# A linear-attention kernel with a sine-gated feed-forward: alpha's load on another queue, w_in in other pieces, the opening's copies and batch 1's steps dealt out anew

## The chip, the cores and the metric

The kernel runs on one core of a Trainium2 chip. A core has five engines that run side by side, each through its own list of instructions in order: TensorE (PE in the profile; PEld is its loading of weights), VectorE (DVE), ScalarE (ACT), GpSimd (POOL) and SyncE (SP). They wait for each other through semaphores. SP, ACT and POOL can also issue DMA transfers, which 16 DMA engines carry out. The metric is the device time of one execution in microseconds (us). Times inside the execution are counted from the start of the profiled span.

## The reference

```python
def _attn_ref(q, k, v):                       # batch 8, heads 8, sequence 576, head_dim 64
    q_s = softmax of q over head_dim          # exp, then divided by the sum over the last axis
    k_s = softmax of k over the sequence
    kv = np.einsum('bhsd,bhse->bhde', k_s, v)
    return np.einsum('bhsd,bhde->bhse', q_s, kv)

def _moe_ref(x, w_in, w_out, alpha):          # 4608 tokens, d_model 512, d_ff 2048
    h = x @ w_in
    s = np.sin(alpha * h)
    g = h + s * s / (alpha + 1e-09)
    return g @ w_out
```

The first function's result, its heads side by side, gives the 4608 x 512 tokens x of the second. All inputs and the output are float32; the matmuls run in bfloat16.

## The kernel before, in words

A batch's 576 tokens lie on 64 partitions with 9 tokens (j) each; two heads share the 128 partitions, so q, k and v of a batch are tiles of 128 x 4 x 9 x 64. They are loaded and worked on in two halves of the heads (ii = 0, 1).

For each batch ACT takes the exponentials of q and k (`exp_half`, `exp_q`, `exp_k`, L119), one engine casts v to bfloat16 beside a column of ones (`cast_v0`, `cast_v1`, `cast_v`), and q is normalized by sums (tensor_reduce, reciprocal) and a product (`norm_q0`, `norm_q`). TensorE multiplies k and v (`kv_mm`, L174, 36 small matmuls for a half), DVE divides by the column that the ones gave (`kv_norm`, L184 and L185: kvr, kbd), TensorE turns q over (`q_transpose_ii`, L201: tp) and multiplies it with kv (`attn_x`, L218). The result is copied to xT, tokens along the free axis.

The feed-forward runs over 9 tiles of 512 tokens. For each of 16 blocks of 128 hidden columns, `mm_h` (L263) adds four matmuls, over four blocks of 128 rows of w_in in the order KO = 0, 2, 1, 3. `sine` (L269) makes sin(alpha h) on ACT; the square is taken by ACT (A, L271), POOL (P, L273) or DVE (D, L275), and `combine` (L279) on DVE adds it to h and writes g. Then `mm_o` (L283) multiplies g and w_out, 64 matmuls a tile, and `evac_o` (L295, L298) copies the sums and stores them.

The order on each engine is the order of the lines, written by hand (`manual_schedule`). PSUM banks come from pools named by letters: a, b and l of two banks each, and k of one double one. A bank is written anew when its last reader is done.

In the opening SP issues q, k, q, v, k of batch 0 (L308, halves), ACT alpha (L313). POOL waits for k's first half (the copy `held`, L340), issues v's second half in two pieces (5 and 4 of the 9 tokens), w_in in six ranges of columns, each by two DMAs of 64 partitions (`load_win`, L109), and the first half of w_out (L112); these DMAs cast float32 to bfloat16. TensorE runs warm-up matmuls until there is work. Then comes tile 0, which needs batch 0 alone. Within its 16 blocks, SP and POOL issue the later loads (`late`, L455): after block 6 q's first half of batch 1, after 8 and 10 w_out's blocks 8 to 12 and 12 to 14, after 13 q's second half and k and v of batch 1. A one-column copy on DVE (L443) to the tile that q's load overwrites keeps that load from starting sooner.

The 64 output matmuls of tile 0 (`o_quad`) are an iterator; `take(os, n)` lets the next n run. Batch 1's attention steps stand between them: `norm_q` (first product on POOL, L153, second on DVE), `held` and w_out's blocks 14 to 16 behind it (L469, L470), the casts of v (first half on ACT, second on DVE, L474), two `transpose_q1` (L482), two `kv_mm` with `kv_norm`, two `x_half` (L491). DMAs of each batch's ninth token of q (q8, L497) and of batch 2 follow. From tile 1 on the order is the same before and after the change.

Of the kernel before, what the change touches and what calls it, by code (L numbers as in the profile page):

```python
# [15 lines left out]
F32 = mybir.dt.float32  # L16
# [7 lines left out]
def kernel(  # L24
# [14 lines left out]
    nc = tc.nc  # L39
# [41 lines left out]
    win_v = moe_w_in.rearrange("(c x d) n -> x d c n", x=2, c=4)  # L81
# [24 lines left out]
    def load_win(c0, c1, k0=0, k1=4):  # L106
        n, kk = slice(c0, c1), slice(k0, k1)
        for x in range(2):
            nc.gpsimd.dma_start(out=win[64 * x:64 * x + 64, kk, n], in_=win_v[x][:, kk, n])  # L109
# [88 lines left out]
    def q_transpose_ii(b, ii, j0, j1, tp):  # L198

        for j in range(j0, j1):  # L200
            nc.tensor.transpose(tp[:, j - j0], A["qn", b][:, ii, j], identb)  # L201
# [111 lines left out]
    nc.scalar.dma_start(out=alpha_rows, in_=moe_alpha.rearrange("(no ni) -> no ni", ni=128))  # L313
# [14 lines left out]
    tpa = warm[:, 0, 0:nN]  # L328
    nc.tensor.transpose(tpa, alpha_rows, ident[0:nN, 0:nN])
    DVE_CP(alpha_sb, tpa)  # L330
    nc.vector.reciprocal(inva_sb, alpha_sb)
# [3 lines left out]
    def cast_v0(ii, j0, j1, eng):  # L335
        vv = vb[0].rearrange("p j (i c) -> p i j c", i=4)
        eng(vv[:, 2 * ii:2 * ii + 2, j0:j1, 0:D], staged["v", 0][:, ii::2, j0:j1])
# [5 lines left out]
    for c0, c1 in ((0, 256), (256, 512), (512, 768), (768, 1024), (1024, 1536), (1536, 2048)):  # L343
        load_win(c0, c1)
# [3 lines left out]
    def warm_up(n):  # L348

        for _ in range(n):  # L350
            nc.tensor.matmul(warm, identb, A["qe", 0][:, 0:4, 0:128], start=True, stop=True)
# [32 lines left out]
    warm_up(1)  # L384
    kv_norm(0, 0, 1)
    tp1 = ps_l.tile([128, 8, 128], BF16, name="tp", tag="l")
    q_transpose_ii(0, 1, 0, 8, tp1)
    cast_v0(1, 0, 5, DVE_CP)
    cast_v0(1, 5, 9, ACT_CP)
# [3 lines left out]
    DVE_CP(xT[:, 0, 0:MF], xp[0])  # L393
    ACT_CP(xT[:, 2, 0:MF], xp[1])
    ACT_CP(A["qT", 0][:, 1, 0:8], tp1)
    nc.scalar.activation(zero, zero, AX.Sin)
    kv_mm(0, 1, ps_k, split=True)
    kv_norm(0, 1, 2)
    for ki in range(2):
        for ni in range(2):  # L400
            mm_h(0, ni, ki, ki + 1)
    xp = [bank("l") for _ in range(2)]
    attn_x(0, 1, 0, 8, xp)
    for x in range(2):
        DVE_CP(xT[:, 2 * x + 1, 0:MF], xp[x])
    for ki in range(2):
        for ni in range(2, 4):
            mm_h(0, ni, ki, ki + 1)
# [29 lines left out]
    with ES:  # L438
# [16 lines left out]
        late = {6: lambda: load_q1(0), 8: lambda: load_wout(8, 12), 10: lambda: load_wout(12, 14), 13: lambda: (load_q1(1), load_kv1())}  # L455
# [9 lines left out]
        take(os, 46)  # L465
        for ii in range(2):
            exp_half("q", 1, ii, 8)
        norm_q(1, [GP, V], 8)
        GP_CP(held, staged["k", 1][:, 0, 0, 0:1])  # L469
        load_wout(14, 16)  # L470

        def cast_v1(ii, eng):
            vv = vb[1].rearrange("p j (i c) -> p i j c", i=4)
            eng(vv[:, 2 * ii:2 * ii + 2, :, 0:D], staged["v", 1][:, ii::2])  # L474

        exp_half("k", 1, 0)
        cast_v1(0, ACT_CP)
        exp_half("k", 1, 1)
        def transpose_q1(ii):
            tp = ps_h[0].tile([128, 8, 128], BF16, name="tp", tag="a")  # L480
            q_transpose_ii(1, ii, 0, 8, tp)
            DVE_CP(q_tile(1)[:, ii, 0:8], tp)  # L482

        transpose_q1(0)
        take(os, 4)
# [6 lines left out]

        kv_mm(1, 0, ps_k, split=True)
        kv_norm(1, 0, 1)
        for b in range(2):
            DVE_CP(q8[:, 0, b, 0:1], zero)
            nc.sync.dma_start(out=q8[:, :, b], in_=src_view(q, b)[:, :, 8 * D:J * D])  # L497
        load_batch(2)
        cast_v1(1, DVE_CP)
        take(os, 4)  # L500
        x_half(0)
        take(os, 2)
        transpose_q1(1)
        kv_mm(1, 1, ps_k, split=True)
        kv_norm(1, 1, 2)
        take(os, 5)
# [186 lines left out]
```

## Time and profile before

| what | us |
|---|---|
| median of 3 runs (lowest, highest) | 283.63 (282.67, 283.71) |
| the profiled execution, its own time | 283.53 |
| its span, first to last instruction | 281.7 |
| TensorE busy | 268.6 |
| ACT, DVE, POOL busy | 224.1, 185.4, 83.5 |
| TensorE busy in 0 to 14 us | 8.08 |
| in 14 to 20 us | 5.71 |
| in 35 to 40 us | 4.35 |
| in 40 to 45 us | 4.39 |
| in 45 to 50 us | 5.00 |

```profile
PE   2999989999999999999999999999999999999994
DMA  7999989996699129811991199125011111111143
```

These two lines cut the span into 40 slices of 7.04 us. A digit is the busy share of a slice in tenths, 9 for 90% or more: for TensorE above, for the mean of the 16 DMA engines below. The granted clock of TensorE was 1.00 throughout. DMA lines in this document give the time from a DMA's issue to its landing; "KB" of a casting load counts the bfloat16 that it writes, half of what it reads.

### The profile page before, as it was taken

Reading aid. Unit: us, or ns where it says so; the run is one execution under the profiler, and the core shown is the slowest. Engines: PE = TensorE matmul, PEld = TensorE weight load, DVE = VectorE, ACT = ScalarE, POOL = GpSimd, SP = SyncE. Lnnn points to the kernel's source line nnn. Section 1 sums busy time; section 2 is a strip of 40 time slices with the busy share of each in tenths; the row PEclk is TensorE's granted clock in tenths of the full one; section 3 lists DMA queues with packets and bytes.
Section 4 is the critical chain, followed back from the end, with each engine's and each line's share of the span. In section 5 each row is a group of like instructions: output and inputs, shape, how many; then the busy total and the mean of one; then the engine's idle time right before and its main releaser. Section 6 shows DMA issues by size and latency. Waiting matters only on the chain.

```text
span 281.7 us, 4930 instructions
## 1 busy us (share of the span) xinstructions
PE 268.6 (95%) x1890; PEld 124.2 (44%) x1919; DVE 185.4 (66%) x280; ACT 224.1 (80%) x320; POOL 83.5 (30%) x80
## 2 busy tenths in 40 slices
PE   2999989999999999999999999999999999999994
PEld 1444444444444444444544444444444444444443
DVE  3868658799868767766866677567675555555412
ACT  4989466999588999899989998999877777777400
POOL 1989410777666550115003500341000000000000
PEclk9999999999999999999999999999999999999999
DMA  7999989996699129811991199125011111111143
GB/s 260 308 187 230 296 288 310 360 329 252 142 171 396 62 61 326 316 37 40 277 381 43 37 249 403 32 57 123 1 36 40 37 37 37 40 38 42 41 106 74
DMA packets 39128, 45.82 MB, mean 163 GB/s; under 512 B 17072, under 2 KB 22464, under 8 KB 39104
## 3 DMA queue, kind: packets, MB, share of 16 engines
q1 hardware_dynamic: 33360, 40.57, 46.6%
q0 software_dynamic: 5552, 4.79, 10.2%
q8 instruction: 15, 0.25, 0.3%
q10 hardware_dynamic: 192, 0.14, 0.2%
q14 instruction: 9, 0.07, 0.1%
HBM read 36.71 MB, written 9.44 MB: 164 GB/s over the span
## 4 chain that ended last, share of the span: by engine, by line
PE 85%; DMA 5%; DVE 4%; ACT 2%; issue 2%; POOL 1%; SPq 0%; ACTq 0%
PE op L283 38%; PE hp L263 37%; DMA st_v<-in_v_dram 3%; PE kvp L174 2%; PE lp L263 2%; DMA st_q<-in_q_dram 1%; POOL s L273 1%; PE op L263 1%; PE op L663 1%; ACT s L269 1%; PE hp L218 1%; PE kvp L263 1%; DVE qs L364 1%; DVE qn L366 1%; PE xp L218 1%
## 5 line engine op out<-in xcount | busy, mean ns | idle before, releaser
L279 DVE SCALAR_TENSOR_TENSOR g<-s,inva_sb,hp 128x512 bf16<-128x512 f32 x128 | 94.5, 745 | 58.8 <-ACT s L271 53.3
L263 PE MATMUL hp<-xT,win 128*128 128x512 bf16 x505 | 127.4, 379 | 0.7 <-DVE kvr L184 0.3
L283 PE MATMUL op<-wout,g 128*128 128x512 bf16 x478 | 121.0, 379 | 1.6 <-issue 1.1
L269 ACT ACTIVATE s<-hp,alpha_sb 128x512 f32<-128x512 f32 x128 | 86.2, 682 | 23.3 <-PE hp L263 21.9
L263 PEld LDWEIGHTS <-win 128*128 128x128 bf16 x576 | 55.9, 98 | 68.0 <-issue 1.7
L283 PEld LDWEIGHTS <-g 128*128 128x128 bf16 x560 | 53.2, 98 | 64.7 <-issue 2.3
L271 ACT ACTIVATE s<-s 128x512 f32<-128x512 f32 x112 | 70.5, 630 | 3.6
L273 POOL TENSOR_TENSOR s<-s 128x512 f32<-128x512 f32 x29 | 30.1, 1056 | 21.8 <-ACT s L269 21.8
L153 POOL TENSOR_TENSOR qn<-qe,qs 128x1152 bf16<-128x1152 bf16 (+1 forms) x12 | 25.1, 2111 | 34.0 <-DVE qs L147 25.3
L295 DVE COPY o<-op 128x512 f32<-128x512 f32 (+2 forms) x33 | 21.8, 660 | 10.2 <-PE op L283 7.9
L138 POOL CAST vb<-st_v 128x1152 bf16<-128x1152 f32 x12 | 14.7, 1259 | 44.7 <-DMA st_v<-in_v_dram 44.7
L119 ACT ACTIVATE qe<-st_q 128x1152 bf16<-128x1152 f32 (+2 forms) x18 | 17.7, 1024 | 6.2 <-DMA st_q<-in_q_dram 6.0
L119 ACT ACTIVATE ke<-st_k 128x1152 bf16<-128x1152 f32 x16 | 17.9, 1151 | 0.9 <-DMA st_k<-in_k_dram 0.9
L146 DVE TENSOR_REDUCE qs<-qe 128x36 f32<-128x2304 bf16 x5 | 12.8, 2551 | 8.3 <-ACT qe L119 8.3
L119 ACT ACT_TABLE_LOAD x7 | 9.0, 1283 | 1.3 <-PEq L677 1.2
L283 PE MATMUL hp<-wout,g 128*128 128x512 bf16 x31 | 8.8, 379 | 0.1
L283 PE MATMUL lp<-wout,g 128*128 128x512 bf16 x30 | 8.6, 380 | 0.2 <-issue 0.2
L174 PEld LDWEIGHTS <-ke 64*64 64x64 bf16 x576 | 5.8, 106 | 5.3 <-issue 2.1
L174 PE MATMUL kvp<-vb,ke 64*64 64x65 bf16 x576 | 6.9, 194 | 1.1 <-ACT vb L474 0.8
L263 PE MATMUL lp<-xT,win 128*128 128x512 bf16 x31 | 7.5, 379 | 0.1
L109 POOL DMA_DIRECT2D win<-in_moe_w_in_dram x12 | 7.4, 701 | 0.0
L231 DVE CAST xT<-xp 128x1024 bf16<-128x1024 f32 (+1 forms) x7 | 7.4, 1065 | 0.0
(86 smaller groups left out, 133.5 us busy)
## 6 DMA issues: line engine op xcount, KB each, us to landing
out_dram<-o SPq DMA_DIRECT2D x70, 128.0 KB, 2.4
st_q<-in_q_dram SPq DMA_DIRECT2D x6, 1152.0 KB, 6.2
st_k<-in_k_dram SPq DMA_DIRECT2D x6, 1152.0 KB, 8.6
st_v<-in_v_dram SPq DMA_DIRECT2D x6, 1152.0 KB, 11.1
st_k<-in_k_dram SPq DMA_DIRECT2D x4, 576.0 KB, 7.3
st_q<-in_q_dram SPq DMA_DIRECT2D x4, 512.0 KB, 5.9
st_v<-in_v_dram SPq DMA_DIRECT2D x3, 576.0 KB, 8.7
wout<-in_moe_w_out_dram POOLq DMA_DIRECT2D x3, 512.0 KB, 10.4
```

Of the source, the lines that this page charges most:

```text
L119: nc.scalar.activation(dst[:, :, ii * 128:(ii + 1) * 128].rearrange("p j (x d) -> p x j d", x=2), src[:, ii::2], AX.Exp)
L138: engs[ii](vv[:, 2 * ii:2 * ii + 2, :, 0:D], staged["v", b][:, ii::2])
L146: nc.vector.tensor_reduce(qs, A["qe", b].rearrange("p j (i d) -> p j i d", i=4), axis=AXL.X, op=ALU.add)
L153: engs[ii % len(engs)].tensor_tensor(qn[:, ii, 0:j1].rearrange("p j (x d) -> p j x d", x=2), qe[:, ii], part.unsqueeze(3).to_broadcast([12 ...
L174: nc.tensor.matmul(kvp[64 * x:64 * x + 64, e, ii * 65:(ii + 1) * 65], ke[r, j, h * 64:(h + 1) * 64], vt[r, j, h * 65:(h + 1) * 65], start= ...
L263: nc.tensor.matmul(hp, win[:, KO[k], ni * 128:(ni + 1) * 128], xT[:, KO[k], t * MF % NX:t * MF % NX + MF], start=(k == 0), stop=(k == 3))
L269: nc.scalar.activation(s, hp, AX.Sin, scale=alpha_sb[:, ni:ni + 1])
L271: nc.scalar.activation(s, s, AX.Square)
L273: nc.gpsimd.tensor_tensor(s, s, s, op=ALU.mult)
L279: nc.vector.scalar_tensor_tensor(G[t][:, ni], in0=s, scalar=inva_sb[:, ni:ni + 1], in1=hp, op0=ALU.mult, op1=ALU.add)
L283: nc.tensor.matmul(acc, G[t][:, ni, j * 128:(j + 1) * 128], wout[:, ni, :], start=(ni == 0), stop=(ni == nN - 1))
L295: eng(o[:, cols], acc)
```

## The change

Four things are changed.

- Alpha's load is issued by SP after the five loads of batch 0, where ACT issued it first. Its transpose on TensorE moves from the start to behind the third group of warm-up matmuls, its copy from DVE to ACT, and the reciprocal (inva_sb) to behind `kv_norm` of the second half.
- w_in comes by 128 partitions in 8 DMAs: rows' blocks 0 and 2 of columns 0 to 256 and 256 to 512, then blocks 1 and 3 of columns 0 to 512, then all rows of four ranges of 256 columns and of the last 512. The first matmuls of tile 0 follow that: block of columns 0 and 1 with row block 0, block 0 with row block 2, and behind `attn_x` of the second half the five others of blocks 0 to 3.
- In the opening both pieces of v's second half are cast by DVE, and DVE also copies q's second transposes; ACT copies both x of the first half and one of the second, and loads the sine's table after that.
- For batch 1, each half of v is cast by ACT (5 tokens) and POOL (4). q is normalized on DVE alone, its transposes come after 42 output matmuls (46 before) and ahead of the second half of v, and all steps are placed anew between the output matmuls. q's second half, k and v are loaded after block 12 of tile 0 (13 before).

```diff
@@ -78,7 +78,7 @@
     def src_view(t, b):
         return t[b].rearrange("(i e) (p j) d -> (e p) i (j d)", e=2, j=J)
 
-    win_v = moe_w_in.rearrange("(c x d) n -> x d c n", x=2, c=4)
+    win_v = moe_w_in.rearrange("(c p) n -> p c n", c=4)
     wout_v = moe_w_out.rearrange("(no ni) d -> ni no d", ni=128)
     out_v = out.rearrange("(b p j) d -> b j p d", b=B, j=J)
 
@@ -103,10 +103,8 @@
         load("k", k, b)
         load("v", v, b)
 
-    def load_win(c0, c1, k0=0, k1=4):
-        n, kk = slice(c0, c1), slice(k0, k1)
-        for x in range(2):
-            nc.gpsimd.dma_start(out=win[64 * x:64 * x + 64, kk, n], in_=win_v[x][:, kk, n])
+    def load_win(c0, c1, cc=slice(0, 4)):
+        nc.gpsimd.dma_start(out=win[:, cc, c0:c1], in_=win_v[:, cc, c0:c1])
 
     def load_wout(n0, n1):
         nc.gpsimd.dma_start(out=wout[:, n0:n1, :], in_=wout_v[:, n0:n1, :])
@@ -310,7 +308,7 @@
 
     for n, t, ii in (("q", q, 0), ("k", k, 0), ("q", q, 1), ("v", v, 0), ("k", k, 1)):
         load0(nc.sync, n, t, ii, 0, 8 if n == "q" else J)
-    nc.scalar.dma_start(out=alpha_rows, in_=moe_alpha.rearrange("(no ni) -> no ni", ni=128))
+    nc.sync.dma_start(out=alpha_rows, in_=moe_alpha.rearrange("(no ni) -> no ni", ni=128))
     make_identity(nc, ident)
     DVE_CP(identb, ident)
     zero = singles.tile([128, 1], F32, name="zero")
@@ -325,10 +323,6 @@
 
     tp0 = ps_h[0].tile([128, 8, 128], BF16, name="tp", tag="a")
     warm = ps_h[0].tile([128, 4, 128], F32, name="warm", tag="a")
-    tpa = warm[:, 0, 0:nN]
-    nc.tensor.transpose(tpa, alpha_rows, ident[0:nN, 0:nN])
-    DVE_CP(alpha_sb, tpa)
-    nc.vector.reciprocal(inva_sb, alpha_sb)
 
 
 
@@ -340,8 +334,12 @@
     GP_CP(held, staged["k", 0][:, 0, 0, 0:1])
     load0(GP, "v", v, 1, 0, 5)
     load0(GP, "v", v, 1, 5, 9)
-    for c0, c1 in ((0, 256), (256, 512), (512, 768), (768, 1024), (1024, 1536), (1536, 2048)):
-        load_win(c0, c1)
+    for c in range(2):
+        load_win(256 * c, 256 * c + 256, slice(0, 4, 2))
+    load_win(0, 512, slice(1, 4, 2))
+    for c in range(2, 6):
+        load_win(256 * c, 256 * c + 256)
+    load_win(1536, 2048)
     for c in range(2):
         load_wout(4 * c, 4 * c + 4)
 
@@ -382,30 +380,32 @@
     warm_up(2)
     kv_mm(0, 0, ps_k, split=True)
     warm_up(1)
+    tpa = warm[:, 0, 0:nN]
+    nc.tensor.transpose(tpa, alpha_rows, ident[0:nN, 0:nN])
     kv_norm(0, 0, 1)
     tp1 = ps_l.tile([128, 8, 128], BF16, name="tp", tag="l")
     q_transpose_ii(0, 1, 0, 8, tp1)
+    ACT_CP(alpha_sb, tpa)
     cast_v0(1, 0, 5, DVE_CP)
-    cast_v0(1, 5, 9, ACT_CP)
+    cast_v0(1, 5, 9, DVE_CP)
+    DVE_CP(A["qT", 0][:, 1, 0:8], tp1)
 
     xp = [bank("b") for _ in range(2)]
     attn_x(0, 0, 0, 8, xp)
-    DVE_CP(xT[:, 0, 0:MF], xp[0])
-    ACT_CP(xT[:, 2, 0:MF], xp[1])
-    ACT_CP(A["qT", 0][:, 1, 0:8], tp1)
-    nc.scalar.activation(zero, zero, AX.Sin)
+    for x in range(2):
+        ACT_CP(xT[:, 2 * x, 0:MF], xp[x])
     kv_mm(0, 1, ps_k, split=True)
     kv_norm(0, 1, 2)
-    for ki in range(2):
-        for ni in range(2):
-            mm_h(0, ni, ki, ki + 1)
+    nc.vector.reciprocal(inva_sb, alpha_sb)
+    for ni, ki in ((0, 0), (1, 0), (0, 1)):
+        mm_h(0, ni, ki, ki + 1)
     xp = [bank("l") for _ in range(2)]
     attn_x(0, 1, 0, 8, xp)
     for x in range(2):
-        DVE_CP(xT[:, 2 * x + 1, 0:MF], xp[x])
-    for ki in range(2):
-        for ni in range(2, 4):
-            mm_h(0, ni, ki, ki + 1)
+        (ACT_CP, DVE_CP)[x](xT[:, 2 * x + 1, 0:MF], xp[x])
+    nc.scalar.activation(zero, zero, AX.Sin)
+    for ni, ki in ((1, 1), (2, 0), (2, 1), (3, 0), (3, 1)):
+        mm_h(0, ni, ki, ki + 1)
 
     def h_slot(t, ni, sq, lag):
         hp = mm_h(t, ni, 2 if ni < (4, 1, 0)[min(t, 2)] else 0)
@@ -452,7 +452,8 @@
                     nc.sync.dma_start(out=staged[n, 1][:, ii::2].rearrange("p i j d -> p i (j d)"),
                                       in_=src_view(t, 1)[:, ii::2])
 
-        late = {6: lambda: load_q1(0), 8: lambda: load_wout(8, 12), 10: lambda: load_wout(12, 14), 13: lambda: (load_q1(1), load_kv1())}
+        late = {6: lambda: load_q1(0), 8: lambda: load_wout(8, 12), 10: lambda: load_wout(12, 14),
+                12: lambda: (load_q1(1), load_kv1())}
         for ni in range(nN):
             h_slot(0, ni, "DPPAPPAPPAAPPAPD"[ni], lag)
             flush(lag, 1)
@@ -462,27 +463,16 @@
 
         accs = [bank(kind) for kind in "bbll"]
         os = o_quad(0, accs, [DVE_CP, ACT_CP, DVE_CP, DVE_CP])
-        take(os, 46)
-        for ii in range(2):
-            exp_half("q", 1, ii, 8)
-        norm_q(1, [GP, V], 8)
-        GP_CP(held, staged["k", 1][:, 0, 0, 0:1])
-        load_wout(14, 16)
-
-        def cast_v1(ii, eng):
+
+        def cast_v1(ii):
             vv = vb[1].rearrange("p j (i c) -> p i j c", i=4)
-            eng(vv[:, 2 * ii:2 * ii + 2, :, 0:D], staged["v", 1][:, ii::2])
-
-        exp_half("k", 1, 0)
-        cast_v1(0, ACT_CP)
-        exp_half("k", 1, 1)
-        def transpose_q1(ii):
+            for j0, j1, eng in ((0, 5, ACT_CP), (5, 9, GP_CP)):
+                eng(vv[:, 2 * ii:2 * ii + 2, j0:j1, 0:D], staged["v", 1][:, ii::2, j0:j1])
+
+        def transpose_q1(ii, eng):
             tp = ps_h[0].tile([128, 8, 128], BF16, name="tp", tag="a")
             q_transpose_ii(1, ii, 0, 8, tp)
-            DVE_CP(q_tile(1)[:, ii, 0:8], tp)
-
-        transpose_q1(0)
-        take(os, 4)
+            eng(q_tile(1)[:, ii, 0:8], tp)
 
         def x_half(ii):
             xp = [bank("a") for _ in range(2)]
@@ -490,20 +480,46 @@
             for x in range(2):
                 (ACT_CP, DVE_CP)[x](xT[:, 2 * x + ii, MF:2 * MF], xp[x])
 
+        def q1_sums(ii):
+            part, src = qs1[:, :, 2 * ii:2 * ii + 2], qe1[:, ii]
+            nc.vector.tensor_reduce(part, src, axis=AXL.X, op=ALU.add)
+            nc.vector.reciprocal(part, part)
+
+        def q1_norm(ii):
+            part = qs1[:, :, 2 * ii:2 * ii + 2]
+            nc.vector.tensor_tensor(A["qn", 1][:, ii, 0:8].rearrange("p j (x d) -> p j x d", x=2), qe1[:, ii],
+                                    part.unsqueeze(3).to_broadcast([128, 8, 2, D]), op=ALU.mult)
+
+        take(os, 42)
+        for ii in range(2):
+            exp_half("q", 1, ii, 8)
+        qe1 = A["qe", 1][:, 0:8].rearrange("p j (ii x d) -> p ii j x d", ii=2, x=2)
+        A["qn", 1] = att1.tile([128, 2, J, 2 * D], BF16, name="qn")
+        qs1 = small.tile([128, 8, 4], F32, name="qs1")
+        GP_CP(held, staged["k", 1][:, 0, 0, 0:1])
+        load_wout(14, 16)
+        q1_sums(0)
+        q1_norm(0)
+        q1_sums(1)
+        exp_half("k", 1, 0)
+        cast_v1(0)
+        transpose_q1(0, DVE_CP)
+        exp_half("k", 1, 1)
+        q1_norm(1)
+        take(os, 10)
         kv_mm(1, 0, ps_k, split=True)
         kv_norm(1, 0, 1)
+        transpose_q1(1, DVE_CP)
         for b in range(2):
             DVE_CP(q8[:, 0, b, 0:1], zero)
             nc.sync.dma_start(out=q8[:, :, b], in_=src_view(q, b)[:, :, 8 * D:J * D])
         load_batch(2)
-        cast_v1(1, DVE_CP)
+        cast_v1(1)
         take(os, 4)
         x_half(0)
-        take(os, 2)
-        transpose_q1(1)
         kv_mm(1, 1, ps_k, split=True)
         kv_norm(1, 1, 2)
-        take(os, 5)
+        take(os, 4)
         x_half(1)
         exp_to(A["qe", 1][:, J - 2:J], q8)
         nc.scalar.activation(zero, zero, AX.Sin)
```

## The prediction

> **What bounds the kernel now.** I read the busy times first, then the chain in order of time, then the timeline of TensorE where it has holes, and last the DMA shares of those stretches.
>
> ```profile
> PE 268.6 (95%) x1890; PEld 124.2 (44%) x1919; DVE 185.4 (66%) x280; ACT 224.1 (80%) x320; POOL 83.5 (30%) x80
> 30.30 8.71 DMA st_v<-in_v_dram
> 39.03 1.18 ACT vb L474
> 38.81 0.59 PE L283 MATMUL hp<-wout,g 128*128 128x512 bf16 x2
> 40.25 0.48 PE L174 MATMUL kvp<-vb,ke 64*64 64x65 bf16 x36 [0.85 <-ACT vb L474]
> 42.02 0.77 DVE L474 CAST vb<-st_v 128x1152 bf16<-128x1152 f32 x1 [0.62 <-DMA st_v<-in_v_dram]
> 43.26 0.48 PE L174 MATMUL kvp<-vb,ke 64*64 64x65 bf16 x36
> 45.85 0.38 PE L263 MATMUL kvp<-xT,win 128*128 128x512 bf16 x1
> ```
>
> TensorE is busy 95% of the span. Matmuls of 512 columns start 0.216 us apart when nothing waits (16 from 28.00 to 31.45), and from 45.85 on they do so almost without a break; the end (266 to 281.7) is one accumulation and a store. So the change can win only before 45.85: in the opening, and in batch 1's part (37 to 46 us), where TensorE runs dry from 39.24 (38.81 plus two starts) to 40.25 and loses about 0.8 us more up to 45.85. The chain blames v of batch 1: first half landed at 39.01, second at 42.00.
>
> ```profile
> core 0: us, PE busy (x) PEld busy (x) DVE busy (x) ACT busy (x) POOL busy (x), PEclk, DMA share, GB/s
> 11.00:17.00 6.00, 5.15 (x66) 2.38 (x67) 3.67 (x9) 5.07 (x8) 5.93 (x10) 1.00 1.37 178
> 18.00:26.00 8.00, 7.95 (x38) 3.62 (x37) 6.95 (x11) 7.85 (x14) 7.16 (x8) 1.00 1.24 205
> 29.00:32.00 3.00, 3.00 (x16) 1.36 (x14) 3.00 (x7) 2.69 (x3) 0.89 (x1) 1.00 1.24 209
> 33.00:39.00 6.00, 5.95 (x34) 2.94 (x34) 2.85 (x5) 2.22 (x2) 2.86 (x3) 1.00 1.05 406
> ```
>
> The last two columns are the point. The DMA engines' share is over 1 from 3 us to 41 us: first q, k, v of batch 0, then w_in, w_out 0 to 8, w_out 8 to 14 with batch 1's loads behind them. (GB/s counts bytes written, so a casting load of 205 reads 410.) The issue time in the chain, 30.30, is then not the cause; the bytes ahead are.
>
> **The opening.** Alpha's load leaves ACT (issue 0.46 us at 0.74) for the sixth place on SyncE. ACT gains nothing: its first exponential waits for q, landed 4.91. Alpha (8 KB) now lands behind the second k half (10.50), by my estimate at 10.6; its transpose stands after the last warm-up matmul (10.81, 0.39 long), so the wait is nothing and the price is one 0.25 us matmul ahead of q's second transposes, 0.1 us net since those waited for DVE until 11.20. At worst it lands with the second v piece (11.95): 0.75.
>
> ```profile
> 13.10 1.02 ACT L395 COPY qT<-tp 128x1024 bf16<-128x1024 bf16 x1
> 14.34 0.41 PE L218 MATMUL lp<-qT,kbd 64*64 64x512 bf16 x4
> 14.79 1.29 DVE L405 CAST xT<-lp 128x512 bf16<-128x512 f32 x2 [1.14 <-PE lp L218]
> 17.64 1.03 PE L263 MATMUL kvp<-xT,win 128*128 128x512 bf16 x4
> ```
>
> DVE: the 640-wide v cast ends at 12.26 as before; the 512-wide one (its 640 took 0.74, so 0.6) to 12.85; qT copy 0.69 (row L482, same shape) to 13.54; kvr and kbd 0.45 to 14.0. ACT: k until 12.22, alpha 0.2, two xT copies of 0.58 to 13.6. Then x of the second half starts at 14.2 instead of 14.34, its two copies run side by side (ACT to 15.2, DVE to 15.35) instead of 1.29 on DVE, and the five matmuls in between end at 15.7. The next eight need the w_in piece of rows 1 and 3, fourth in POOL's queue: by the landings of before (12.57, 13.25, then 1.29 for 512-wide columns) about 14.6. So column block 4 starts at 15.7 + 8 x 0.216 = 17.4, 0.2 earlier than 17.64. ACT's table load moves from 14.15 to 15.2 and ends, with the dummy sine, at 16.7; the first sine at 16.55 becomes 16.7. Cover: the combine of block 12 ends at 29.28 and TensorE wants its bank at 29.73, 0.45 ahead; 0.2 + 0.15 fit. Bounds: -0.45 to +0.75, most likely -0.2.
>
> w_in: 12 issues (0.69 us each) become 8 of 0.66 to 0.8 (w_out's, with as many rows, take 0.81), so POOL is through a us sooner, and waits for ACT's sines at 17.90 anyway. Of its bytes 0.26 MB (512 rows x 256 columns x 2) go from the rate of 512-wide columns (205) to that of 256-wide (178): 0.2 us more of a full DMA.
>
> **Batch 1, the loads.** q's second half, k and v are issued after block 12 instead of 13: their gate (L443, 29.20) now follows block 11's combine (ends 28.28), so about 28.5, with ACT's shift: 0.8 earlier, five DMAs on SyncE, nothing else queued there. Their price lies between -0.8 (they land earlier by all of it) and +0.2 (a full DMA serves the same bytes, w_in costing 0.2 more). By the share of 1.24 in 29 to 32 us I take +0.2: second v half 42.2, first 39.2.
>
> **Batch 1, the work.** q's first product moves from POOL (1.91 us) to DVE (1.22), between the sums: ready at 34.6, transposed after 42 matmuls of the output instead of 46 (36.9 instead of 37.9); no wait. The second product starts when the copy of the first transposes is done, 38.6 to 39.8. v's halves are split, ACT 640 wide (between 0.61 for 512 and 1.17 for 1152: 0.72), POOL 512 wide (1.17 for 1152 undisturbed, so 0.55). Here DVE and POOL meet:
>
> ```profile
> 67.89 1.97 DVE L153 TENSOR_TENSOR qn<-qe,qs 128x1152 bf16<-128x1152 bf16 x1
> 68.59 3.40 POOL L138 CAST vb<-st_v 128x1152 bf16<-128x1152 f32 x2
> ```
>
> This product takes 1.38 alone (1.22 x 9/8) and here waited for POOL's until 68.6; POOL's first cast took 2.29 instead of 1.17, from 68.59 to 70.88, one us beyond DVE's end. So POOL's first piece waits for DVE until 39.8 and ends at 40.4, against ACT's 39.9: 0.5 us on the first kv product, which ends at 40.7.
>
> The Trainium skill has this as a rule against the change ("SBUF — State Buffer", section "SBUF: two separate sides"): a DVE instruction with two SBUF inputs and a GpSimd one hold a shared port pair exclusively, and the loser fully blocks. The rows above agree. By the rule both halves could lose; but beside the second v half DVE has only copies out of PSUM, so the sum would stay at the 0.5 already in it.
>
> Then q's second transposes 0.45 (41.2), their copy on DVE to 42.1, four matmuls to 42.05, x 0.35: TensorE is ready for the second kv product at 42.5. It needs v: 42.2 + 0.04 + 0.72 = 42.96. From there kv 0.41, four matmuls 0.86, x 0.35, four 0.86: 2.48, and block 0 of the next tile starts at 45.45 instead of 45.85. All that was in between 42 and 45.85 (two matmuls, second transposes, a wait of 0.14 for the xT copy) is done before v. The last w_out piece (issued at 36.93 behind `held`, 6.1 us to landing, 43.07) gets no earlier in a full DMA, 43.3, and is wanted at 43.37: it covers, barely, and caps any further gain.
>
> **The sum.** 0.40 us won at 45.85. The opening's 0.2 is lost in the wait for v, as would be a loss there up to 0.46. Downstream: q8's loads are issued 0.5 later (behind the qT copy on DVE), land near 45.3, and ACT reads them at 45.5 (45.79 before); batch 2's loads follow 0.5 later and are used from 61 us on. Nothing else moves. The profiled execution took 283.53 (span 281.7 and 1.8 around it); its median of runs is 283.63. 283.53 - 0.40 = 283.1.
>
> **The rivals.**
> - Issue bound. If v lands 0.8 earlier with its issue, as the chain has it, the second kv product starts when TensorE is ready, 42.5, or 42.1 if POOL is not blocked: 282.7 to 282.3. For it: SyncE's loads had 395 of 401 GB/s at 33 us, so they may push w_out 12 to 14 (wanted at 38.6, landed 34.45) behind them. Against it: the share over 1 throughout.
> - The last w_out piece ahead of v (slower). Its issue hangs on k's first half; if that comes earlier by passing w_out, 0.5 MB of reads enters POOL's queue while v's second half is under way, and costs at most 1.28 us at 410 GB/s, of which some 0.4 is paid now. Second v half 42.9, next tile 46.2: 283.9. It decides from a landing of 42.6 on.
> - No effect: v's cast and the opening save what the extra w_in time and POOL's block cost, 283.5.
> - The opening breaks: alpha or the ACT shift cost more than the 0.66 that is covered in all; 0.75 and a stalled bank would give 284 to 285.
>
> The Trainium skill speaks for the second ("DMA: Bandwidth & Descriptors", section "Queues, rings and completion order"): an engine goes round robin over the queues that have work. By it the sum would be near 283.9. No window here isolates that order.
>
> **How the numbers follow.** Forecast (282.8 to 283.5, with no effect in it) 0.55; issue bound 0.20; w_out ahead of v 0.17; opening 0.08. The range takes in 282.3 below and 283.9 above, and the 0.1 to 0.4 by which single runs of before differ (282.67 to 283.71): 282.2 to 284.3. A measurement tells 0.5% (1.4 us) from no change; the whole hole is about that, so faster by more 0.08 (from the first rival, with luck in the runs), slower by more 0.11 (the last and the worst of the second), within 0.81.
>
> **What would show it.** Right: kv of batch 1 waits for ACT's cast of v near 43.0 and block 0 of tile 1 starts near 45.4; v's second half lands at 42.0 to 42.4; POOL's first cast takes over 0.9. Wrong: v lands near 41.2, or after 42.6; TensorE waits for alpha; a stall for banks at 20 to 30 us.

## The result, and the profile after

The changed kernel takes 282.62 us (median of 22 runs, 282.06 to 283.69) where the kernel before took 283.56 on the same chip (22 runs): a ratio of 0.9963, interval 0.9949 to 0.9977. On another chip the pair gave 282.66 (12 runs) and 282.82 (35), ratio 0.9989 (0.9971 to 1.0007), which takes in no change. So it is faster by 0.4% on the first chip, and by a tenth of a per cent that the noise covers on the other; both are within the half per cent that the prediction called no change. What differs between the chips is the kernel before: 283.56 on the first, 282.82 to 282.86 on three others. The profiled execution of the changed kernel took 282.79 us, 0.74 less than that of before; its span is 280.98 (281.73 before). That execution of before (283.53), from which the prediction starts too, lies at the first chip's median and 0.7 above those of the three others, so that the two profiles stand for the first chip's difference and not for the others'.

The page's line of busy times:

```profile
PE 267.7 (95%) x1890; PEld 124.0 (44%) x1919; DVE 185.5 (66%) x279; ACT 223.8 (80%) x322; POOL 81.3 (29%) x77
```

The chain that ended last, in order of time (start, length, what):

```profile
8.90 5.92 DMA win<-in_moe_w_in_dram
14.83 0.05 issue
14.87 1.90 PE hp L261 x8
...
29.41 12.43 DMA st_v<-in_v_dram
41.84 0.02 issue
41.86 0.75 ACT vb L470
42.60 0.04 issue
42.65 0.48 PE kvp L172 x32
```

It is the same chain as before: v of batch 1, its cast, the kv product. The load is issued at 29.41 (31.32 before) and lands at 41.84 (42.00): 1.9 us bought 0.16. The cast is 0.75 long where DVE's took 0.77 and ACT's 1.18, and now nothing stands between it and the product. Before, the cast ended at 42.79 (42.02 + 0.77) and the product started at 43.26, because the second transposes stood ahead of it on TensorE:

```profile
42.72 0.61 PE L201 MATMUL tp<-identb,qn 128*128 128x128 bf16 x8
```

TensorE of the changed kernel from the product on:

```profile
42.65 0.48 PE L172 MATMUL kvp<-vb,ke 64*64 64x65 bf16 x36 [1.24 <-ACT vb L470]
43.11 1.02 PE L281 MATMUL hp<-wout,g 128*128 128x512 bf16 x4
44.06 0.41 PE L216 MATMUL hp<-qT,kbd 64*64 64x512 bf16 x4
44.63 0.81 PE L281 MATMUL lp<-wout,g 128*128 128x512 bf16 x3 [0.16 <-issue]
45.28 1.03 PE L261 MATMUL kvp<-xT,win 128*128 128x512 bf16 x4
```

TensorE has done all else and stands idle for 1.24 us until v is cast; tile 1 starts at 45.28 instead of 45.85. The windows of before, asked again:

```profile
core 0: us, PE busy (x) PEld busy (x) DVE busy (x) ACT busy (x) POOL busy (x), PEclk, DMA share, GB/s
11.00:17.00 6.00, 5.50 (x66) 2.40 (x65) 3.59 (x8) 5.01 (x10) 3.86 (x7) 1.00 1.31 176
...
29.00:32.00 3.00, 3.00 (x16) 1.35 (x15) 3.00 (x5) 1.79 (x2) 0.00 (x0) 1.00 1.21 236
33.00:39.00 6.00, 5.91 (x33) 2.80 (x32) 3.82 (x5) 2.83 (x3) 1.52 (x3) 1.00 1.06 383
```

The DMA share stays over 1. The opening (11 to 17 us) has TensorE busy for 5.50 instead of 5.15.

### The profile page after: what moved, and what is told of

Same layout as the page of the kernel before. It is cut to its first block, busy times and chain, and to the rows that moved or that the text cites. A ratio compares the mean times of both kernels' runs of the same rounds, so it can differ in the third digit from the quotient of the medians.

```text
span 281.0 us, 4925 instructions
## 1 busy us (share of the span) xinstructions
PE 267.7 (95%) x1890; PEld 124.0 (44%) x1919; DVE 185.5 (66%) x279; ACT 223.8 (80%) x322; POOL 81.3 (29%) x77
## 4 chain that ended last, share of the span: by engine, by line
PE 85%; DMA 8%; POOL 2%; issue 1%; SPq 1%; ACT 1%; DVE 1%; ACTq 0%
PE op L281 38%; PE hp L261 38%; DMA st_v<-in_v_dram 4%; DMA win<-in_moe_w_in_dram 2%; PE lp L261 2%; PE kvp L172 2%; DMA st_k<-in_k_dram 2%; PE op L261 1%; PE op L679 1%; POOL s L271 1%; PE kvp L261 1%; PE hp L216 1%; PE xp L216 1%; POOL st_v L306 1%; DVE g L277 1%
## 5 line engine op out<-in xcount | busy, mean ns | idle before, releaser
L151 POOL TENSOR_TENSOR qn<-qe,qs 128x1152 bf16<-128x1152 bf16 x11 | 23.2, 2127 | 29.5 <-DVE qs L145 24.4
L349 PE MATMUL warm<-qe,identb 128*128 128x512 bf16 x10 | 4.1, 554 | 5.0 <-ACT qe L117 5.0
```

Source lines behind the costliest of these rows:

```text
L151: engs[ii % len(engs)].tensor_tensor(qn[:, ii, 0:j1].rearrange("p j (x d) -> p j x d", x=2), qe[:, ii], part.unsqueeze(3).to_broadcast([12 ...
```

## The experiments

Twelve runs on three chips; each chip's runs share one set of runs of the kernel before (35 each: 282.86, 282.82 and 282.82 us). The order here is by question. "v" is the landing of batch 1's last v half, on the middle one of its 16 DMA engines and on the slowest; the product waits for the slowest. "Loss" is how much longer than 0.216 us TensorE takes from the start of block 11's last matmul in tile 1 to the four small transposes behind it, which turn q8.

| profiled execution | loads issued after block | column block 4, tile 0 | v, middle | v, slowest | tile 1 starts | loss | span |
|---|---|---|---|---|---|---|---|
| before | 13 | 17.64 | 39.78 | 42.00 | 45.85 | 0.20 | 281.73 |
| after | 12 | 16.61 | 40.12 | 41.84 | 45.28 | 0.06 | 280.98 |
| after, run again | 12 | 16.88 | 39.95 | 41.62 | 45.03 | 0.05 | 280.69 |
| batch 1 alone | 12 | 17.72 | 39.57 | 41.33 | 44.77 | 0.94 | 281.37 |
| opening alone | 13 | 16.73 | 39.72 | 41.04 | 45.25 | 0.20 | 281.06 |
| loads after block 13 | 13 | 16.49 | 39.57 | 40.74 | 44.15 | 0.44 | 280.25 |
| the same, run again | 13 | 17.12 | 39.81 | 41.16 | 44.63 | 0.92 | 281.18 |
| alpha first on ACT | 12 | 17.81 | 40.68 | 42.83 | 46.23 | 0.06 | 281.91 |
| alpha on ACT, later | 12 | 16.60 | 39.89 | 41.01 | 44.41 | 0.30 | 280.32 |
| w_out early | 12 | 18.10 | 41.70 | 43.22 | 46.63 | 0.40 | 282.65 |
| wide w_in | 12 | 20.06 | 41.66 | 43.65 | 47.05 | 0.81 | 283.51 |
| cast by ACT alone | 12 | 16.87 | 39.77 | 42.13 | 45.97 | 0.05 | 281.64 |
| q8 sooner | 12 | 16.92 | 40.48 | 41.92 | 45.37 | 0.05 | 281.05 |
| q8 sooner, block 13 | 13 | 16.93 | 40.25 | 41.78 | 45.25 | 0.05 | 280.94 |

The table closes: in all fourteen the span is the start of tile 1 + the loss + 235.6 (235.61 to 235.67). In the eleven with the new order and the cast in two parts, the second kv product starts 0.80 to 0.81 behind v's slowest engine and tile 1 another 2.59 to 2.66 behind that. So three things make all of the difference between these executions: when v lands on its slowest engine, how it gets from there to the product, and the loss. The opening enters only through the first.

**Which part brings the gain?** The first run is the kernel before with the change's batch 1, the second the changed kernel with batch 1 of before.

```diff
-        late = {..., 13: lambda: (load_q1(1), load_kv1())}
+        late = {..., 12: lambda: (load_q1(1), load_kv1())}
...
-        def cast_v1(ii, eng):
+        def cast_v1(ii):
...
+        take(os, 42)
```

> The opening of before (alpha first on ACT, w_in by 64 partitions, copies as before) with batch 1's steps of the changed kernel. Theory (batch 1 is bound by the DMA bytes up to v's second half and the last w_out piece): v's second half lands near 42.0 as before, the second kv product follows its cast at 42.8 instead of 43.26, tile 1 starts at 45.3 to 45.5 (before 45.85, changed 45.28): 0.4 to 0.5 us less than before, ratio 0.998 to 0.9986. Rival (the gain is the opening's, 17.64 to 16.61 at column block 4, carried through): tile 1 at 45.8 to 46.0, ratio 0.9995 to 1.001.

```diff
-                12: lambda: (load_q1(1), load_kv1())}
+        ... 13: lambda: (load_q1(1), load_kv1())}
...
+        take(os, 46)
...
-        def cast_v1(ii):
+        def cast_v1(ii, eng):
```

> The opening of the changed kernel with batch 1's steps, and the loads after block 13, of before. Theory: column block 4 of tile 0 at 16.6 as in the changed kernel, but v's second half lands at 41.8 to 42.0 all the same and tile 1 starts at 45.6 to 45.8: ratio 0.999 to 1.0. Rival (the opening's 1.0 us carries): tile 1 at 44.8 to 45.0, ratio 0.9965.

Batch 1 alone: 283.17 us, ratio to before 1.0012 (1.0001 to 1.0024). Opening alone: 282.79, 0.9998 (0.9986 to 1.0011). Neither half wins by itself, and the first run missed what was expected of it in the time and at tile 1 (44.77). The opening by itself starts column block 4 at 16.73, 0.9 us sooner, and ends with the time of before, as expected, though v landed and tile 1 started sooner than that (41.04, 45.25). TensorE's timeline of this kernel:

```profile
39.65 0.48 PE L172 MATMUL kvp<-vb,ke 64*64 64x65 bf16 x36 [1.16 <-ACT vb L474]
...
42.12 0.61 PE L199 MATMUL tp<-identb,qn 128*128 128x128 bf16 x8
42.65 0.48 PE L172 MATMUL kvp<-vb,ke 64*64 64x65 bf16 x36
```

The hole ahead of the first kv product has grown from 0.85 to 1.16: 0.31 of the 0.91 won in the opening is waited away for v's first half. The other 0.60 stays in this execution, because that half landed 0.60 sooner (38.41 against 39.01); the median of the runs shows no gain. And though v's second half landed at 41.04, the product starts 1.61 later, because in the old order the second transposes stand ahead of it and wait for a copy. Batch 1 alone has the 0.81, and its tile 1 is early, but it lost 0.94 at block 11, which the next but one question is about.

**Does the issue or do the bytes set v's landing?** The changed kernel with its loads issued after block 13, as before:

```diff
-                12: lambda: (load_q1(1), load_kv1())}
+                13: lambda: (load_q1(1), load_kv1())}
```

> The changed kernel with q's second half, k and v of batch 1 loaded after block 13 again. Theory (a full DMA serves the same bytes whenever they are issued): v's second half lands at 41.8 +- 0.25, tile 1 at 45.3 +- 0.2, ratio as the changed kernel's, 0.9963. Rival (issue bound): loads issued 1.0 later land 1.0 later, v at 42.8, tile 1 at 46.2, ratio 0.9995.

282.72 us, ratio 0.9999 (0.9987 to 1.0011); run again on another chip 282.96, 0.9997 (0.9979 to 1.0014). v is issued at 30.55 and 30.86 instead of 29.41 and 29.93, and lands no later: 39.57 and 39.81 on the middle engine against 40.12 and 39.95. (On the slowest, 40.74 in the first run is earlier than the 41.8 expected.) The counterpart puts more bytes ahead of v, by loading w_out's last piece with the one before it:

```diff
-... 10: lambda: load_wout(12, 14),
+... 10: lambda: load_wout(12, 16),
...
-        GP_CP(held, staged["k", 1][:, 0, 0, 0:1])
-        load_wout(14, 16)
```

> The changed kernel with w_out's blocks 14 to 16 loaded with 12 to 14 after block 10, not behind k's first half: 0.5 MB of reads more ahead of batch 1's loads. Theory: q's second half, k and v land 1.28 us later on the median engine (41.2 to 41.4 for v's second half, the last at 42.8 to 43.2), the second kv product starts at 43.6 to 44.0, nothing waits for w_out, tile 1 starts at 46.1 to 46.5, ratio 0.003 above the changed kernel's. Rival (v is not bound by the bytes ahead): tile 1 at 45.3 or earlier, ratio the changed kernel's or lower.

284.01 us, ratio 1.0041 (1.0019 to 1.0064), 1.35 above the changed kernel on this chip. v moves by 1.6 us on the middle engine, to 41.70, with an issue at 30.84. Not all of it is the piece's: in this execution TensorE also waited 1.34 us for a w_in piece, which this edit doesn't touch, and w_in's last piece landed at 24.16, 0.7 later than in after.

```profile
14.00 1.03 PE L261 MATMUL hp<-xT,win 128*128 128x512 bf16 x4 [0.16 <-PE lp L216]
16.36 0.82 PE L261 MATMUL hp<-xT,win 128*128 128x512 bf16 x3 [1.34 <-DMA win<-in_moe_w_in_dram]
```

Two other executions had w_in's last landing as late (24.15, alpha first; 24.16, q8 sooner with block 13) and v on the middle engine at 40.68 and 40.25. Against these the piece moves v by 1.0 to 1.45. So the bytes ahead move v, and an issue that is 0.9 to 1.1 later does not while the DMA engines stay full (a share of 1.24 in 29 to 32 us before, 1.21 after).

**Where is the gain lost when tile 1 starts early?** The changed kernel and the one with block 13 were run again on another chip.

> The changed kernel once more, beside other kernels on their chip, since the kernel before took 283.56 on the first chip and 282.86 on the next. If the gain is the kernel's, ratio 0.9963 +- 0.0014 again. If it hangs on which DMA engine falls behind, which may differ by chip and execution, the ratio is nearer 1 (0.998 to 1.000), and v's second half lands elsewhere than at 41.84: by the profiles so far 40.7 to 42.8 on the slowest engine, while the median engine is done at 39.6 to 40.1.

> The changed kernel with the loads after block 13 again, beside the changed kernel. In its first profile v landed at 40.74 and tile 1 started at 44.15, a us ahead of the changed kernel's, while its ratio was 0.9999. Theory (full DMA, the slowest engine decides by chance): the median engine finishes v's second half at 39.4 to 39.8, ratio within 0.0015 of the changed kernel's. Rival (issuing earlier, among w_out's packets, costs DMA time): the median engine 0.3 to 0.5 earlier than in the changed kernel in this pair too, ratio 0.001 to 0.002 lower. Rival (issue bound): v later by 1.0 and ratio 0.003 higher.

The ratios are 0.9989, the reading nearer to 1 of the two expected, and 0.9997. The timeline of the second, ACT and TensorE:

```profile
44.63 1.03 PE L261 MATMUL kvp<-xT,win 128*128 128x512 bf16 x4
...
45.36 0.72 ACT L117 ACTIVATE qe<-q 128x256 bf16<-128x256 f32 x2 [0.76 <-DMA q<-in_q_dram]
...
53.27 1.89 PE L261 MATMUL lp<-xT,win 128*128 128x512 bf16 x7
55.92 0.38 PE L539 MATMUL tp<-identb,qe 128*128 128x128 bf16 x4 [0.76 <-DVE g L277]
```

ACT waits 0.76 us for q8's second load, landed at 45.26. Behind its exponentials stand the table load and tile 1's first sines, and TensorE runs on without them until its banks are used up at block 11: the profile names DVE's combine as what it waits for, and the wait is the same 0.76. In the other runs too the loss follows ACT: in all twelve executions with batch 1's new order it is 0.19 to 0.21 us more than ACT's start on q8's exponentials lies behind the start of tile 1. ACT idled ahead of them in six: 0.78 us (batch 1 alone), 0.28 and 0.76 (block 13, twice), 0.14 (alpha later), and also, with a late tile 1, 0.24 (w_out early) and 0.66 (wide w_in). These are the six in which q8's second load landed 3.41 us or more behind v's slowest engine; in the six others it landed 2.93 or less behind, and ACT did not wait. So the distance between the two landings decides, and not when tile 1 starts. In five of the six ACT starts 0.10 to 0.11 behind the landing. In batch 1 alone it starts 0.43 behind it, and the profile names a copy of DVE there: some 0.3 of its 0.78 is not q8's, and no run shows whose it is. An early v is not kept: with the loads after block 13, run again, tile 1 starts 0.65 before that of after and the span is longer by 0.20.

q8's loads wait on DVE behind the copy of the second transposes. Two kernels have their gates ahead of that copy, one of them with loads after block 13:

```diff
-        transpose_q1(1, DVE_CP)
         for b in range(2):
             DVE_CP(q8[:, 0, b, 0:1], zero)
             nc.sync.dma_start(out=q8[:, :, b], in_=src_view(q, b)[:, :, 8 * D:J * D])
+        transpose_q1(1, DVE_CP)
```

> The changed kernel, with the two copies that gate q8's loads and the loads themselves ahead of the second transposes' copies on VectorE: q8's loads are issued some 0.6 us sooner, behind the gate of the first transposes as before. Theory (the wait for v sets the start of tile 1, and q8's second load caps what an early start is worth): q8's second load lands at 44.0 to 44.6 or some 3.0 us behind the landing of v's second half; ScalarE reads it without a wait, and TensorE loses under 0.1 us ahead of tile 1's block 11 even where tile 1 starts at 44.2 to 45.0. The second transposes wait a little for VectorE: at most +0.1 on the second kv product, which waits for the cast anyway. Time: that of the changed kernel where tile 1 starts late, up to 0.5 lower where it starts early; mean -0.1 to -0.3 (282.4 to 282.6 where the changed kernel takes 282.7). Rival (q8's landing follows from the bytes, not from the issue): it lands where it did, and the stall stays.

> The changed kernel, with both q8's gates ahead of the second transposes' copies and batch 1's loads issued after block 13 instead of 12. Theory (landing of v set by the bytes, not by the issue; q8's second load no longer late): v's second half lands where the changed kernel has it (40.7 to 41.8 by the slowest engine, 39.6 to 40.1 by the middle one), tile 1 starts at 44.2 to 45.0, and no more than 0.1 is lost ahead of block 11. Time 282.2 to 282.7, the lowest of these kernels. Rival (a later issue costs): v lands 0.5 to 0.9 later and the time is 283.0 or more.

282.88 us, ratio 0.9991 (0.9976 to 1.0006), and 282.29, 0.9978 (0.9965 to 0.9992). The second is the lowest of all, but the intervals of the two overlap, and they stand beside the changed kernel's 0.9963 and 0.9989: better than it is not shown. The first missed its time. In both profiled executions tile 1 started at 45.25 or later, where nothing is lost in the changed kernel either, so they don't show that the stall is gone; q8's second load landed 2.1 and 2.9 us behind v, as in the four other executions without a wait.

**What does the cast in two parts bring?**

```diff
-            for j0, j1, eng in ((0, 5, ACT_CP), (5, 9, GP_CP)):
+            for j0, j1, eng in ((0, 9, ACT_CP),):
```

> The changed kernel, with each half of v cast by ScalarE alone (nine row blocks in one instruction instead of five on ScalarE beside four on GpSimd). A cast of five blocks takes 0.73 us, so nine take some 1.2 to 1.3. Theory (v's landing, then the cast, set the second kv product): second kv product 1.45 us behind the landing of v's second half by the slowest of its engines instead of some 0.8 to 1.0, the first product likewise; tile 1 starts 0.4 to 0.5 later relative to v's landing; the time +0.3 to +0.5 against the changed kernel (283.0 to 283.2) where v's landing is the same. Rival (the cast is not on the path, since the last w_out piece at 42 to 43 covers it): no more than +0.1.

```profile
42.15 1.17 ACT L470 CAST vb<-st_v 128x1152 bf16<-128x1152 f32 x1 [0.24 <-DMA st_v<-in_v_dram]
...
43.37 0.48 PE L172 MATMUL kvp<-vb,ke 64*64 64x65 bf16 x36 [2.06 <-ACT vb L470]
...
45.97 1.03 PE L261 MATMUL kvp<-xT,win 128*128 128x512 bf16 x4
```

The product starts 1.24 behind v, as before's did (1.26), not 0.81; behind v's landing, tile 1 is later by the same 0.43. So the cast is on the path, and against one by ACT alone its split is worth 0.43 us in an execution. Before's cast of this half, by DVE, took 0.77, as long as the split one; there the second transposes were the limit, and that they now come ahead of v is what makes 1.26 into 0.81. (A cast by DVE in the new order was not tried; its copy to xT ran from 41.49 to 42.18 in after.) The time did not show the 0.43: 282.73 us, ratio 0.9995 (0.9982 to 1.0007), where 283.0 to 283.2 was expected. A ratio's interval of a quarter of a per cent is 0.7 us wide, more than this term.

**Why is q earlier in the opening?** Alpha back at the head of ACT's queue, all else as changed; and alpha on ACT's queue, but issued behind the first exponentials of q and k (5.77 us).

```diff
-    nc.sync.dma_start(out=alpha_rows, in_=moe_alpha.rearrange("(no ni) -> no ni", ni=128))
+    nc.scalar.dma_start(out=alpha_rows, in_=moe_alpha.rearrange("(no ni) -> no ni", ni=128))
```

> The changed kernel with alpha's load first on ACT's queue again; its transpose stays where it is. In the changed kernel q's first half landed at 4.28 (before: 4.91). If alpha's early packets cause that, q lands at 4.9 here and column block 4 of tile 0 starts at 17.0 to 17.2 (16.61). Theory: TensorE waits 1.24 us for v before the second kv product, so tile 1 still starts at 45.2 to 45.45 and the ratio is 0.996 to 0.997. Rival (the opening's time carries): tile 1 at 45.9, ratio 0.9985.

> The changed kernel, with alpha's load on ScalarE's queue, but issued only after the first exponential (q's first half has landed by then). It tells whether alpha delays the opening because it lies in ScalarE's queue or because its 512-byte packets are moved first. Theory (early packets): q's first half lands at 4.3 to 4.5 as in the changed kernel, column block 4 of tile 0 starts at 16.5 to 16.9, time as the changed kernel (within 0.1 %). Rival (the queue, or the issue on ScalarE, costs): q lands as in the changed kernel, but the steps behind on ScalarE's queue land 0.4 to 0.6 late, and column block 4 starts at 17.5 to 17.8; the time is still as the changed kernel's, since the wait for v absorbs it.

282.92 us, ratio 1.0006 (0.9993 to 1.0019), and 282.50, 0.9985 (0.9974 to 0.9996). The DMA issues of the first 8 us, alpha first, with KB each and the median us to landing:

```profile
st_q<-in_q_dram SPq DMA_DIRECT2D x2, 512.0 KB, 4.8
...
alpha_rows<-in_moe_alpha_dram ACTq DMA_DIRECT2D x1, 8.0 KB, 2.3
```

and alpha later:

```profile
st_q<-in_q_dram SPq DMA_DIRECT2D x2, 512.0 KB, 4.4
...
alpha_rows<-in_moe_alpha_dram ACTq DMA_DIRECT2D x1, 8.0 KB, 4.4
```

q's first half landed at 4.74 and at 4.31. Over all executions it is 4.54 to 4.91 in the three with alpha at the head (before, batch 1 alone, alpha first) and 4.28 to 4.53 in the others: 0.3 us by the means. So it is the 8 KB moved early that cost, and not the queue: on ACT's queue later (one execution) they delay nothing. Column block 4 starts at 17.81 and 16.60, but 0.77 of that difference is a wait for the w_in piece of row blocks 1 and 3, which landed at 16.03 with alpha first and anywhere from 14.54 to 16.32 in the kernels with these pieces: alpha's part is no more than q's. Alpha first missed the ratio (0.996 to 0.997) and the tile 1 (45.2 to 45.45) that were expected. The two times don't judge the opening either, since v's landing (42.83 and 41.01) lies further apart than the opening could make it.

**Do the narrow first pieces of w_in pay?** The first 512 columns in two DMAs of 512 columns instead of three:

```diff
-    for c in range(2):
-        load_win(256 * c, 256 * c + 256, slice(0, 4, 2))
-    load_win(0, 512, slice(1, 4, 2))
...
+    for r in range(2):
+        load_win(0, 512, slice(r, 4, 2))
```

> The changed kernel with w_in's first columns in two pieces of 512 columns (row blocks 0 and 2, then 1 and 3), then two ranges of 256 and two of 512. 256-wide columns go at 178 GB/s, 512-wide at 205: by that 0.58 us of a full DMA is saved. Theory: the first tile's matmuls start 0.2 to 0.4 later (w_in's first piece lands at 12.8), w_out 0 to 4 lands 0.4 to 0.6 earlier, v's second half 0.4 to 0.6 earlier on the median engine, tile 1 at 44.7 to 44.9, ratio 0.0015 below the changed kernel's. Rival (the opening's start decides): tile 1 0.2 to 0.4 later, ratio 0.001 above.

283.27 us, ratio 1.0017 (0.9985 to 1.0049), unclear by the median. The first piece landed at 14.62, 1.8 later than expected, and TensorE stood still for 2.07 us. Windows of this kernel, the columns as above:

```profile
12.50:14.70 2.20, 0.13 (x13) 0.04 (x2) 0.84 (x4) 0.24 (x1) 0.95 (x2) 0.95 1.24 189
14.70:17.00 2.30, 2.00 (x7) 0.51 (x9) 0.22 (x1) 0.26 (x1) 0.00 (x0) 0.50 1.44 200
17.00:20.00 3.00, 2.97 (x12) 1.29 (x12) 0.72 (x2) 2.78 (x5) 0.00 (x0) 0.85 1.26 207
```

Behind the hole the granted clock is 0.50 for over two microseconds, so that column block 4 starts at 20.06. Of these 3.45 us against after, 1.8 remain at tile 1 (47.05 against 45.28): the wait for v takes up the rest, although v's own issue (33.10) is late enough to move its landing, since the DMA engines ran short of work (a share of 0.89 in 29 to 32 us).

The single runs explain the wide interval. Five of the twelve, this execution among them, have a mean granted clock of 0.991 to 0.994 and take 284.70 to 285.76 us; the other seven have 0.998 to 1.000 and take 282.59 to 283.27, at most 0.6 above the changed kernel's 282.66 on this chip. So the wide pieces cost most where the clock falls. A mean clock of 0.992 to 0.994 also stands in six of the 105 runs of the kernel before on the three chips (284.05 to 285.57 us), and in none of the changed kernel's 34; where it fell in those six no trace shows.

## Why the prediction held, and where its steps did not

The prediction was 283.1 us with 282.2 to 284.3; 282.62 lies in it, 0.5 below, but under the 282.8 to 283.5 that was given the most weight. The range holds the time of before as well, so that the number alone says little. Against its own profiled execution it summed -0.40 where -0.74 was measured. Of its four signs of being right two came (the product by ACT's cast of v, at 42.65; tile 1 at 45.28) and two did not (v at 41.84, POOL's first cast 0.72 long). Point by point:

- **The bound.** "The issue time in the chain, 30.30, is then not the cause; the bytes ahead are" holds: in eleven executions with the same bytes ahead, issues from 29.41 to 31.32 land within 39.57 and 40.48 on the middle engine, in no order (alpha first, with w_in late, at 40.68), and 256 KB more in front move it by 1.0 to 1.6. It holds while the engines are full: with wide w_in, where their share fell to 0.89 and v was issued at 33.10, v landed at 41.66. The rival of the issue bound gave 282.3 to 282.7, and the median falls there, but by another way: v did not land earlier by its issue.
- **w_out ahead of v.** This rival did not come: the piece landed behind v in all thirteen executions that have it there. "No window here isolates that order" overlooked one: in before's trace from 37 to 39 us, with the piece issued at 36.93, SP's queue has 102.4% of the 16 engines' time and POOL's queue of casting loads 0.6%. The order is not strict, though: in after, SP's and POOL's queues shared the engines from 31 to 34 us (58.4% and 54.5%).
- **v at 42.2.** Of the extra w_in time (+0.2) the middle engine shows +0.3 in this pair (39.78 became 40.12), and by the means of nine executions with the new opening and two with the old one (39.95, 39.68); they scatter by 0.9, so it is not shown. The product waits for the slowest engine, 1.1 to 2.4 us behind the middle, and that varies from execution to execution more than the change moves it: 40.74 to 42.13 over nine executions with the new opening and nothing heavier ahead of v. The 41.84 of the profiled one is a draw, and the text treated one landing as a constant.
- **The cast and the way to tile 1.** 0.04 + 0.72 was 0.81, 2.48 was 2.63. This is where the gain of this pair of executions comes from: v to product 1.26 before, 0.81 after. The step that the prediction named for it is right: the second transposes are done before v. The split cast by itself (0.75 against DVE's 0.77) gives next to nothing of it.
- **The sum.** 0.57 at tile 1 instead of 0.40: 0.16 by v, 0.45 by the way from v to the product, less 0.04 behind it. The other 0.14 is a term that the sum did not have: the kernel before lost 0.20 at block 11 of tile 1, where ACT came to q8's exponentials 0.06 us ahead of tile 1's start (45.79), and after loses 0.06, where ACT is 0.15 ahead (45.13); 0.03 is spread over the rest. In the time of the runs no part of this sum is shown: batch 1 alone, which has the 0.81 too, took 1.0012 of before.
- **The opening.** -0.2 was -1.03, or about -0.9 by the means (w_out early, with its late w_in piece, left out). The step that failed is "ACT gains nothing: its first exponential waits for q, landed 4.91": that landing itself moves, to 4.28, when alpha's load goes. The remaining 0.4, against the 0.2 of the text, belongs to the rest of the opening; no run parts the dealing-out of the copies from the w_in pieces. As predicted, it is lost in the wait for v in the pair of profiles, so that the error cost the forecast nothing.
- **POOL's block.** The mechanism is right, and works both ways. Two kernels' timelines of DVE and POOL, q8 sooner with block 13 first, then block 13:

```profile
38.79 1.21 DVE L490 TENSOR_TENSOR qn<-qe,qs 128x1024 bf16<-128x1024 bf16 x1
38.94 1.54 POOL L470 CAST vb<-st_v 128x512 bf16<-128x512 f32 x1 [0.41 <-DMA st_v<-in_v_dram]
...
40.53 0.32 PE L172 MATMUL kvp<-vb,ke 64*64 64x65 bf16 x16 [0.49 <-POOL vb L470]
```

```profile
37.71 0.62 POOL L470 CAST vb<-st_v 128x512 bf16<-128x512 f32 x1 [0.45 <-DMA st_v<-in_v_dram]
37.92 1.47 DVE L490 TENSOR_TENSOR qn<-qe,qs 128x1024 bf16<-128x1024 bf16 x1
```

  Where DVE's product starts first (in one of them within 0.01), the cast ends 0.47 to 0.49 behind it, in all six executions in which they meet so, and takes up to 1.70 us instead of 0.62; where the cast is first, the product takes 1.37 or 1.47 instead of 1.21. In the profiled execution after they overlapped by 0.24 only (cast 38.43, 0.72 long), so "over 0.9" missed. This is the rule of the Trainium skill ("SBUF — State Buffer", section "SBUF: two separate sides"), that one of the two holds the shared ports for its whole instruction, whoever came first; these rows agree. The price is 0.1 to 0.5 on the first product in four of the six, nothing in two, and is waited away with v's second half.
- **The last w_out piece.** Forecast at 43.3, landed at 43.07, and the first matmul that wants it (43.11) is let go by it. It lands 1.07 to 1.26 behind v's slowest engine in every execution that has it there, and is wanted 1.22 behind (0.81 and the kv product's 0.41), so it comes earlier with v and costs 0.08 at most: it covers, but does not cap the gain as the text had it.
- **What the text had no rival for.** q8's second load was forecast near 45.3 and read at 45.5, "covered". It landed at 44.51 and was read at 45.13 without a wait; but where it lands 3.41 us or more behind v, as in six executions, ACT waits and TensorE pays: in the four in which tile 1 started before 45.0, 0.30 to 0.94 were lost again. In three of these, and for more than half of the fourth's wait, it is this load that takes back what an earlier v brought. The text named the cover and not what it would cost if it went.

What stays open: whether q8's earlier loads remove that cap in the time, why the slowest DMA engine lags by so different an amount, and why the kernel before takes 283.56 us on one chip and 282.82 to 282.86 on three others, so that the pair's ratio is 0.9963 on the first and 0.9989 on another (the intervals meet at 0.9971 to 0.9977). Which change makes the gain in the time is not shown: neither half has it alone.

## What to carry to other kernels

When all DMA engines are full, as here, a load's landing follows from the bytes in front of it and not from its issue, and time won ahead of that wait can be waited away. What counts then is all that stands between the landing and the first use: in the profiled executions, second transposes moved ahead of the landing were worth 0.45 us, and a cast of 1.17 us by one engine in place of 0.74 by two cost 0.43. The time of the runs, with intervals of a quarter of a per cent, shows neither. Look for the next transfer that was hidden by the wait (here 256 KB of q8) before counting on an earlier start. Where a wait ends with the slowest of 16 engines, one trace is one draw: compare the middle engine to see an edit, and several executions to see the time.

## What the runs showed of the hardware that was not expected

- An 8 KB load on a second queue, issued together with the first large one, delayed that one by 0.3 us (4.73 against 4.42 by the means of 3 and 11 executions); issued 5 us later on the same queue, it delayed nothing (4.31, one execution).
- A load's last DMA engine finished 1.1 to 2.4 us behind its middle one (v of batch 1), and the w_in piece of row blocks 1 and 3, the same in eleven of these executions, landed between 14.54 and 16.32.
- A hole of 2.07 us at 12.6 to 14.67 (wide w_in) was followed by a granted clock of 0.50 from 14.50 to 17.91, that is for 3.41 us, while one of 2.06 at 41.3 to 43.37 (cast by ACT alone) left it at 1.00. But for the last of each trace, the recorded stretches of one clock are 3.41, 6.83, 266.24, 269.65 and 273.07 us long: 1, 2, 78, 79 and 80 times 3.413. In the 3.41 us ahead of the fall (11.09 to 14.50) TensorE was busy for 1.20. Counted on in such steps from the first record of its trace, the other hole lies across two of them (39.26 to 42.67 and to 46.08), busy for 2.00 and 2.55. That fits a clock that goes by the work within a step and not by the hole's length; how much work it takes no run here shows. The Trainium skill ("TensorE: Matmul & The Clock Gate", section "Part 1: The HAM clock gate") has the clock fall after an idle window of some 3.4 us, of a free-running counter; the length agrees, but the window ahead of this fall was not idle.
- The clock records begin at 10.34 in before, so its 1.00 is not shown ahead of that: there seven warm-up matmuls of 512 columns took 3.15 us from 5.61 on, some 0.42 us from one to the next, against 0.216 later.
